# The transfers of two hardware DMA queues, tied in one order: a gated-attention and low-rank-mixer kernel

## The chip, the cores and the metric

The kernel runs on one NeuronCore of a Trainium2 chip. The metric is the device time of one execution in microseconds (us); the time before is the median of five executions. A profile of one of these executions shows each instruction of the engines: TensorE (PE, and PEld for its weight loads), VectorE (DVE), ScalarE (ACT), GpSimd (POOL) and SyncE (SP), and the DMA transfers that SP, ACT and POOL issue.

## The reference

Two blocks run one after the other on eight batches of 3136 rows and 256 columns. The first is a gated attention with squared ReLU, the second a low-rank mixer over the sequence with a two-layer network behind it.

```python
scores = (1.0 / S) * z @ z.T            # z: [8, 3136, 64], S = 3136
attn   = np.maximum(scores, 0.0) ** 2
x      = u * (attn @ v)                 # u, v: [8, 3136, 256]
h      = x.T @ U @ V                    # U: [3136, 32], V: [32, 3136]
y      = x + h.T
out    = y + np.maximum(y @ w_ch1, 0.0) @ w_ch2    # 256 -> 1024 -> 256
```

## The kernel before

The 3136 rows of a batch are 24 blocks of 128 rows and a tail of 64 rows (`NT`, `TAIL`). The scores are symmetric, so a block of the score matrix is computed once; where both it and its transpose are wanted, the second is made by a DMA transpose. Work for one batch runs as follows.

- `load_z`, `cast_z` and `tr_z` (lines 895 to 923) bring z in, scale it to bf16 and transpose it into `zT`. In batch 0 the transpose is a matmul, from batch 1 on a DMA transpose on the SP queue: three of eight blocks, and one for the tail.
- `score` (L1025) multiplies two blocks of `zT` into a pair of PSUM banks. `relu_q` (L1040 on ACT, L1042 on DVE) clips it into SBUF tile `q`, `square` (L1046) squares it, `tr_quad` (L1049) transposes some blocks with a DMA on the SP queue.
- `av` (L1053) multiplies the squared scores by v, which `load_v` (L940) and `cast_v` brought in; `gate` (L1086) multiplies the sum by u, which `load_u` (L967, L970) brought in, and gives x. The tail columns go through `copy_o24` (the copy at L888 into `o`) and a transposing matmul (L1078).
- `t1`, `t1s`, `hmm` (L1095, L1112, L1133) are the low-rank part; `uadd`, `ucast`, `utr` (L1144, L888, L1161) make y and transpose it with a DMA; `w1`, `relu1`, `w2`, `outadd`, `store` (L1171 to L1217) are the two-layer network and the stores.
- Only in batch 0, `load_w` (L978 to L993) and `cast_w` bring the weights in, in between: U and V first, then the two layers' weights.

The work around the change is ordered by a planner. `make_plan` plays the whole kernel through with estimated durations, picks an engine for each task and gives a list of tasks, `plan.order`. The kernel then walks that list under `tc.manual_schedule()`, and each engine executes its own instructions in the order in which they were recorded. Loads are issued from the ACT queue (a few early ones from SP), so they stand in one stream with ScalarE's own instructions; all DMA transposes are issued from SP; stores are issued from POOL, those of the last batch from SP.

```python
    plan = make_plan()
    with tc.manual_schedule():
        bufs = Bufs(tc.nc, ctx, tc, u, v, z, moe_U, moe_V, moe_w_ch1, moe_w_ch2, out)
        for t in plan.order:
            t.emit(bufs, t)
```

How the engines' streams interleave is not fixed by this. The recording layer lays all instructions out in one list of its own. A transfer of SP or ACT takes the next of eight semaphores (`DMAHW0` to `DMAHW7`) as its turn in that list comes, whichever of the two queues it is on; the built program shows it. Each transfer raises its semaphore on landing. So that counts stay clear, a queue waits before it issues a transfer until the previous transfer on the same semaphore, the eighth before it in the list, has landed. On ACT everything behind that transfer waits too. The text below calls this the turn wait. There are 733 such transfers: 487 on SP (458 of them transposes) and 246 on ACT.

Of the kernel before, what the change touches and what calls it, by code (L numbers as in the profile page):

```python
# [15 lines left out]
P = 128  # L16
NB, S, D, DQK, R, H = 8, 3136, 256, 64, 32, 1024
NT = 24
TAIL = S - NT * P
# [17 lines left out]
GATE_V = 0  # L37
# [12 lines left out]
class Ref:  # L50
# [4 lines left out]
    def __init__(self, pool):  # L55
        self.pool, self.i, self.n = pool, None, 0
# [757 lines left out]
class Bufs:  # L814


    def __init__(self, nc, ctx, tc, u, v, z, mU, mV, w1, w2, out):
        self.nc = nc
        self.d = dict(u=u, v=v, z=z, U=mU, V=mV, w1=w1, w2=w2, out=out)
        sb = ctx.enter_context(tc.tile_pool(name="sb", bufs=1))  # L820
        ps = ctx.enter_context(tc.tile_pool(name="ps", bufs=1, space=bass.MemoryType.PSUM))

        def many(name, n, shape, dt):
            return [sb.tile(shape, dt, name=f"{name}{i}") for i in range(n)]

        self.q = sb.tile([P, NBLK, P], BF16, name="q")
        self.xc = many("xc", NXC, [P, 4, D], BF16)
        self.x24 = many("x24_", 2, [P, P], BF16)
        self.stg = many("stg", 6, [P, 512], FP32)
        self.us = many("us", 3, [P, 2, D], FP32)  # L830
        self.zbf = many("zbf", 2, [P, 8, P], BF16)
        self.zbt = sb.tile([P, P], BF16, name="zbt")
        self.zT = many("zT", 2, [P, (NT + 1) * P], BF16)
        self.v = many("v", 2, [P, NT + 2, D], BF16)
        self.TJ = many("TJ", 1, [P, (NT + 1) * 64], BF16)
        self.o24 = many("o24_", 1, [P, P], FP32)
        self.u24 = many("u24_", 1, [P, P], FP32)
        self.u32 = many("u32_", 3, [P, 4, D], FP32)
        self.ubf = many("ubf", 1, [P, ND * 4 * P], BF16)
        self.uT = many("uT", 2, [P, ND * 4 * P], BF16)  # L840
        self.ubt = sb.tile([P, P], BF16, name="ubt")
        self.r1 = many("r1_", 7, [P, 2, 512], BF16)
        self.r24 = many("r24_", 1, [P, NH, 192], BF16)
        self.ob = many("ob", 2, [P, 2, D], FP32)
        self.t1sb = many("t1_", 2, [P, D], BF16)
        self.w1b = sb.tile([P, ND, H], BF16, name="w1b")
        self.w2b = sb.tile([P, NH, D], BF16, name="w2b")
        self.Ub = sb.tile([P, NT + 2, R], BF16, name="Ub")
        self.V4 = sb.tile([P, 6 * P], BF16, name="V4")
        self.Vt = sb.tile([P, 192], BF16, name="Vt")  # L850
        self.t1f = many("t1f", 1, [P, D], FP32)
        self.rep = sb.tile([P, P], FP32, name="rep")
        self.pair = [ps.tile([P, 2, 512], FP32, name=f"pair{i}") for i in range(NPAIR)]
        self.acc = [ps.tile([P, 512], FP32, name=f"acc{i}") for i in range(NACC)]
        self.ident = sb.tile([P, P], BF16, name="ident")
        make_identity(nc, self.ident)
        self.identf = sb.tile([P, P], FP32, name="identf")
        nc.vector.tensor_copy(out=self.identf, in_=self.ident)
        nc.vector.memset(self.zbt[64:], 0.0)
        for t in self.v:  # L860
            nc.vector.memset(t[64:, NT, :], 0.0)
            nc.vector.memset(t[:64, NT + 1, :], 0.0)
        nc.vector.memset(self.r24[0], 0.0)
        nc.vector.memset(self.Ub[64:, NT, :], 0.0)
        nc.vector.memset(self.Ub[:64, NT + 1, :], 0.0)
        nc.vector.memset(self.Vt, 0.0)

    def own(self, x):
# [6 lines left out]
            return q.bitcast(FP32).rearrange("p (t d) -> p t d", d=D)  # L875
        return q

    def q_of(self, t):
        return {"SP": self.nc.sync, "POOL": self.nc.gpsimd, "ACT": self.nc.scalar, "DVE": self.nc.vector}[t.eng]

# [5 lines left out]
    def copy(self, t, out, in_):  # L886
        if t.eng == "ACT":
            self.nc.scalar.copy(out=out, in_=in_)  # L888
        elif t.eng == "POOL":
            self.nc.gpsimd.tensor_copy(out=out, in_=in_)  # L890
        else:
            self.nc.vector.tensor_copy(out=out, in_=in_)  # L892


    def load_z(self, t, b, z0, nb, st):
        s = self.stg[st.i]
        if z0 < NT:
            self.q_of(t).dma_start(
                out=s[:, : nb * DQK].rearrange("p (t d) -> p t d", d=DQK), in_=self.rows("z", b, z0, z0 + nb)
            )  # L900
        else:
            self.q_of(t).dma_start(out=s[:TAIL, :DQK], in_=self.d["z"][b, NT * P :, :])

    def cast_z(self, t, z0, nb, st, zbf, h):
        s = self.stg[st.i]
# [10 lines left out]
    def tr_z(self, t, z0, zbf, zT):  # L916
        if z0 < NT:
            o = self.zT[zT.i][:, z0 * P : (z0 + 8) * P].rearrange("p (t r) -> p t r", r=P)
            i = self.zbf[zbf.i].rearrange("p t c -> p (t c)")
        else:  # L920
            o = self.zT[zT.i][:, NT * P :].rearrange("p (t r) -> p t r", r=P)
            i = self.zbt[:, :]
        self.nc.sync.dma_start_transpose(out=o, in_=i)

    def mm_z(self, t, z0, nb, zbf, pr):
        for n in range(nb):
# [10 lines left out]
    def load_v(self, t, b, k, st):  # L937
        s = self.stg[st.i]
        if k < 12:
            self.q_of(t).dma_start(  # L940
                out=s.rearrange("p (t d) -> p t d", d=D), in_=self.rows("v", b, 2 * k, 2 * k + 2)
            )
        else:
            self.q_of(t).dma_start(out=s[:TAIL, :D], in_=self.d["v"][b, NT * P :, :])

    def load_v_bf(self, t, k, v):
        self.q_of(t).dma_start(
            out=self.v[v.i][:, 2 * k : 2 * k + 4, :], in_=self.rows("v", 0, 2 * k, 2 * k + 4)
        )

    def gate_v(self, t, v):
        w = self.v[v.i]
        self.nc.gpsimd.tensor_copy(out=w[:1, NT // 2, :1], in_=w[:1, 2 * GATE_V, :1])

    def cast_v(self, t, k, st, v):
        s = self.stg[st.i]
# [7 lines left out]

    def load_u(self, t, b, c, u):
        if c < NT:
            self.q_of(t).dma_start(out=self.us[u.i], in_=self.rows("u", b, c, c + 2))  # L967
        else:
            for h in range(2):
                self.q_of(t).dma_start(  # L970
                    out=self.u24[u.i][h * TAIL : (h + 1) * TAIL, :],
                    in_=self.d["u"][b, NT * P :, h * P : (h + 1) * P],
                )

    def load_w(self, t, n, g, st):
        s, q = self.stg[st.i], self.q_of(t)
        if n < 4:
            q.dma_start(out=s, in_=self.d["w1"][n // 2 * P : (n // 2 + 1) * P, n % 2 * 512 : (n % 2 + 1) * 512])  # L978
        elif n < 8:
            d = self.d["w2"][(n - 4) * 2 * P : (n - 3) * 2 * P, :]  # L980
            q.dma_start(out=s.rearrange("p (t d) -> p t d", d=D), in_=d.rearrange("(t p) d -> p t d", p=P))
        elif n < 10:
            t0 = (n - 8) * 12
            q.dma_start(
                out=s[:, : 12 * R].rearrange("p (t r) -> p t r", r=R), in_=self.rows("U", None, t0, t0 + 12)
            )
            if n == 9:
                q.dma_start(out=s[:TAIL, 12 * R : 13 * R], in_=self.d["U"][NT * P :, :])
        else:

            c0 = ((n - 10) * 4 + g) * 504
            w = min(504, S - c0)
            q.dma_start(out=s[g * R : (g + 1) * R, :w], in_=self.d["V"][:, c0 : c0 + w])  # L993

    def cast_w(self, t, n, g, st):
        s = self.stg[st.i]
# [49 lines left out]
        self.nc.vector.tensor_tensor(out=o, in0=o, in1=o, op=ALU.mult)  # L1046

    def tr_quad(self, t, src, off, tb, nt):
        self.nc.sync.dma_start_transpose(out=self.q[:, tb.i : tb.i + nt, :], in_=self.cols(src, off, nt * P))  # L1049

    def av(self, t, seg, acc, v, d0, first, last):
        for n, (_, ref, j) in enumerate(seg):
# [101 lines left out]
    def utr(self, t, k, ubf, uT):  # L1154
        if k < 6:
            i = self.own(ubf)
            o = self.own(uT).rearrange("p (t r) -> p t r", r=P)
        else:
            i = self.ubt[:, :]
            o = self.own(uT)[:, :P].rearrange("p (t r) -> p t r", r=P)  # L1160
        self.nc.sync.dma_start_transpose(out=o, in_=i)  # L1161

    def w1(self, t, k, g, pr, uT):
        ps = self.pair[pr.i]
# [46 lines left out]
    def store(self, t, b, k, h, ob):  # L1211
        if k < 6:
            t0 = 4 * k + 2 * h
            self.q_of(t).dma_start(out=self.rows("out", b, t0, t0 + 2), in_=self.ob[ob.i])  # L1214
        else:
            for e in range(2):
                self.q_of(t).dma_start(  # L1217
                    out=self.d["out"][b, NT * P :, e * P : (e + 1) * P],
                    in_=self.ob[ob.i][e * TAIL : (e + 1) * TAIL, 0, :P],
                )  # L1220
# [3 lines left out]
def kernel(  # L1224
# [9 lines left out]
    out: bass.AP,  # L1234
):
    plan = make_plan()
    with tc.manual_schedule():
        bufs = Bufs(tc.nc, ctx, tc, u, v, z, moe_U, moe_V, moe_w_ch1, moe_w_ch2, out)
        for t in plan.order:
            t.emit(bufs, t)  # L1240
# [30 lines left out]
```

## Time and profile before

| what | value |
|---|---|
| median of five executions | 1041.83 us |
| lowest and highest | 1039.83 and 1047.07 us |
| the profiled execution: its own time | 1040.88 us |
| its span in the trace | 1039.1 us |
| its mean granted TensorE clock | 0.998 |
| busy: PE, PEld | 1009.5 us, 747.0 us |
| busy: DVE, ACT, POOL | 597.7 us, 485.8 us, 72.6 us |
| DMA transposes `q<-q` on SP, issue to landing | 364, median 3.9 us |
| loads of v, 256 KB, on ACT, issue to landing | 84, median 3.6 us |

The time of the profiled execution is 1.78 us more than its span, and 0.95 us less than the median. "Busy" does not count the instructions that only wait or that issue a transfer; those stand under the queue's name (ACTq, SPq). An idle time is shown in brackets behind the instruction that ended it, with what released it.

### The profile page before, as it was taken

The numbers are of one execution on the slowest core, as the hardware profiler recorded it, in microseconds if no ns is written. First come the engines' busy times: TensorE is split into PE (matmuls) and PEld (weight loads), VectorE is DVE, ScalarE is ACT, GpSimd is POOL, SyncE is SP. The second block draws the span as 40 slices with busy tenths as digits, with TensorE's granted clock in tenths as the row PEclk, the third lists the DMA queues.
The fourth block names the chain that finished last, engine by engine and source line by source line (L and its number), as shares of the span: only waits on it lengthen the run. The fifth ranks groups of instructions, "written<-read, shape, count | busy, mean of one in ns | idle before, by whom it ended". The sixth has DMA issues, their size and how long they took to land.

```text
span 1039.1 us, 22175 instructions
## 1 busy us (share of the span) xinstructions
PE 1009.5 (97%) x9103; PEld 747.0 (72%) x9177; DVE 597.7 (58%) x1064; ACT 485.8 (47%) x596; POOL 72.6 (7%) x137
## 2 busy tenths in 40 slices
PE   8798999999999999999999999999999999999997
PEld 5477677777777767777777777677777777777765
DVE  7785754746654566646566554754655655652352
ACT  7553455344545355444454444644464454542343
POOL 1140000000000000001000000000000001000000
PEclk9999999999999999999999999999999999999999
DMA  9989999968797899898699886997889888762152
GB/s 209 172 218 220 185 186 206 202 153 168 167 216 169 166 178 197 182 183 173 139 224 188 188 156 139 212 208 167 166 168 207 195 184 153 136 142 80 40 124 78
DMA packets 413990, 177.84 MB, mean 171 GB/s; under 512 B 375712, under 2 KB 379104, under 8 KB 413888
## 3 DMA queue, kind: packets, MB, share of 16 engines
q1 hardware_dynamic: 372880, 96.91, 55.7%
q10 hardware_dynamic: 33408, 56.25, 19.9%
q0 software_dynamic: 7600, 23.27, 7.2%
q8 instruction: 71, 1.16, 0.5%
q14 instruction: 31, 0.25, 0.1%
HBM read 60.70 MB, written 25.69 MB: 83 GB/s over the span
## 4 chain that ended last, share of the span: by engine, by line
PE 89%; DMA 5%; DVE 3%; ACT 1%; issue 1%; ACTq 0%; POOL 0%; SPq 0%; POOLq 0%; DVEq 0%
PE acc L1053 46%; PE acc L1197 16%; PE pair L1171 15%; PE pair L1025 7%; DMA uT<-ubf 2%; PE acc L1063 2%; DVE q L1046 1%; DMA zT<-zbf 1%; PE pair L1133 1%; PE acc L1068 1%; DMA stg<-in_v_dram 1%; DMA q<-q 1%; PE acc L1190 1%; ACT q L1040 1%; PE acc L1095 1%
## 5 line engine op out<-in xcount | busy, mean ns | idle before, releaser
L1053 PE MATMUL acc<-v,q 128*128 128x256 bf16 x4632 | 572.2, 274 | 4.7 <-DVE xc L1086 4.4
L1053 PEld LDWEIGHTS <-q 128*128 128x128 bf16 x4632 | 441.3, 98 | 123.5 <-issue 50.4
L1040 ACT ACTIVATE q<-pair 128x1024 bf16<-128x1024 f32 (+6 forms) x263 | 214.4, 862 | 220.8 <-PE pair L1025 207.6
L1182 ACT ACTIVATE r<-pair 128x1024 bf16<-128x1024 f32 (+1 forms) x191 | 186.5, 1008 | 185.9 <-PE pair L1171 161.8
L1046 DVE TENSOR_TENSOR q<-q 128x1024 bf16<-128x1024 bf16 (+6 forms) x392 | 211.1, 579 | 14.3 <-ACT q L1040 13.5
L1086 DVE TENSOR_TENSOR xc<-acc,us 128x256 bf16<-128x256 f32 x192 | 81.0, 422 | 192.6 <-PE acc L1053 96.7
L1197 PE MATMUL acc<-w2b,r 128*128 128x256 bf16 x1536 | 182.4, 273 | 0.0
L1171 PE MATMUL pair<-uT,w1b 128*128 128x512 bf16 (+1 forms) x716 | 165.7, 350 | 5.7 <-DMA uT<-ubf 2.0
L1197 PEld LDWEIGHTS <-r 128*128 128x128 bf16 x1536 | 149.0, 98 | 24.3 <-issue 4.0
L1042 DVE TENSOR_SCALAR q<-pair 128x768 bf16<-128x768 f32 (+6 forms) x129 | 125.1, 975 | 52.5 <-PE pair L1025 48.2
L1171 PEld LDWEIGHTS <-w1b 128*128 128x128 bf16 x896 | 78.5, 98 | 70.8 <-issue 5.4
L1209 DVE TENSOR_TENSOR ob<-acc,u 128x512 f32<-128x512 f32 (+1 forms) x91 | 60.0, 659 | 86.4 <-PE acc L1197 85.8
L1214 POOL DMA_DIRECT2D out_dram<-ob x84 | 46.7, 556 | 849.2 <-DVE ob L1209 804.9
L1025 PE MATMUL pair<-zT 64*128 64x384 bf16 (+3 forms) x952 | 100.8, 314 | 4.4 <-ACT q L1040 3.1
L1025 PEld LDWEIGHTS <-zT 64*128 64x128 bf16 x952 | 35.8, 95 | 35.1 <-issue 25.6
L1144 DVE TENSOR_TENSOR u<-pair,xc 128x1024 f32<-128x1024 f32 x42 | 50.1, 1218 | 9.6 <-PE pair L1133 9.6
L888 ACT CAST ubf<-u 128x1024 bf16<-128x1024 f32 x23 | 24.0, 1045 | 61.1 <-DVE u L1144 54.1
L892 DVE CAST v<-stg 128x512 bf16<-128x512 f32 (+1 forms) x69 | 28.1, 409 | 18.7 <-DMA stg<-in_v_dram 17.8
L1063 PE MATMUL acc<-v,q 64*128 64x256 bf16 (+1 forms) x168 | 27.0, 277 | 0.0
L912 ACT ACTIVATE zbf<-stg 128x512 bf16<-128x512 f32 (+1 forms) x34 | 19.8, 615 | 10.5 <-DMA stg<-in_z_dram 10.0
L1171 PE MATMUL pair<-q,w1b 128*128 128x512 bf16 (+1 forms) x106 | 22.0, 351 | 1.6 <-DVE q L1144 1.0
L1063 PEld LDWEIGHTS <-q 64*128 64x128 bf16 (+1 forms) x168 | 11.3, 95 | 11.7 <-issue 10.3
(71 smaller groups left out, 242.3 us busy)
## 6 DMA issues: line engine op xcount, KB each, us to landing
us<-in_u_dram ACTq DMA_DIRECT2D x93, 256.0 KB, 3.5
stg<-in_v_dram ACTq DMA_DIRECT2D x84, 256.0 KB, 3.6
out_dram<-ob POOLq DMA_DIRECT2D x84, 256.0 KB, 3.1
q<-q SPq DMA_TRANSPOSE x364, 3.9
stg<-in_z_dram ACTq DMA_DIRECT2D x22, 256.0 KB, 3.2
out_dram<-ob SPq DMA_DIRECT2D x12, 256.0 KB, 2.0
stg<-in_moe_w_ch_dram ACTq DMA_DIRECT2D x8, 256.0 KB, 3.5
stg<-in_v_dram SPq DMA_DIRECT2D x6, 256.0 KB, 3.8
```

Source lines behind the costliest of these rows:

```text
L1025: self.nc.tensor.matmul(out=ps[:, h, pc : pc + w], lhsT=z[a, r * P : (r + 1) * P], rhs=z[a, c0 : c0 + w], start=True, stop=True,)
L1040: self.nc.scalar.activation(out=o, in_=i, func=AF.Relu)
L1042: self.nc.vector.tensor_single_scalar(out=o, in_=i, scalar=0.0, op=ALU.max)
L1046: self.nc.vector.tensor_tensor(out=o, in0=o, in1=o, op=ALU.mult)
L1053: self.nc.tensor.matmul(out=self.acc[acc.i][:, d0 : d0 + D], lhsT=self.q[:, ref.i, :], rhs=self.v[v.i][:, j, :], start=first and n == 0, s ...
L1063: self.nc.tensor.matmul(out=a[:, :D], lhsT=q[r], rhs=v[r, NT + n, :], start=n == 1, stop=n == 0)
L1086: self.nc.vector.tensor_tensor(out=o, in0=i0, in1=i1, op=ALU.mult)
L1144: self.nc.vector.tensor_tensor(out=o, in0=i, in1=x, op=ALU.add)
L1171: self.nc.tensor.matmul(out=o, lhsT=self.w1b[:, e, ht * P : (ht + 1) * P], rhs=r, start=e == 0, stop=e == ND - 1)
L1182: self.nc.scalar.activation(out=o, in_=i, func=AF.Relu)
L1197: self.nc.tensor.matmul(out=self.acc[acc.i][:, w * D : (w + 1) * D], lhsT=self.r1[r1s[ht // 2].i][:, ht % 2, (2 * h + w) * P : (2 * h + w ...
L1209: self.nc.vector.tensor_tensor(out=o, in0=i, in1=x, op=ALU.add)
```

## The change

All transfers of SP and ACT, loads, stores and transposes alike, go through a new method `chain`. It adds an edge from each to the one recorded before it, whichever queue that was on. The edge is of the kind `NoSync`: it orders the two in the recording layer's list and puts no wait on the chip. The eight semaphores thus come round in the order of `plan.order`. POOL is taken out of the manual schedule, and each of its instructions is tied to the one recorded before it on POOL by `keep_in_program_order`.

```diff
-        self.nc = nc
+        self.nc, self.tc, self.last = nc, tc, None
...
+    def dma(self, t, out, in_):
+        i = self.q_of(t).dma_start(out=out, in_=in_)
+        if t.eng == "POOL":
+            self.tc.keep_in_program_order(i)
+        else:
+            self.chain(i)
+
+    def chain(self, i):
+        if self.last is not None:
+            self.tc.add_manual_dep(
+                i.ins, self.last.ins.name, mybir.DependencyInfo(mybir.DependencyClass.NoSync, mybir.DependencyReason.DATA),
+                reason="order of transfers",
+            )
+        self.last = i
...
-            self.nc.gpsimd.tensor_copy(out=out, in_=in_)
+            self.tc.keep_in_program_order(self.nc.gpsimd.tensor_copy(out=out, in_=in_))
...
-            self.q_of(t).dma_start(
+            self.dma(t, 
                 out=s.rearrange("p (t d) -> p t d", d=D), in_=self.rows("v", b, 2 * k, 2 * k + 2)
             )
...
-        self.nc.sync.dma_start_transpose(out=self.q[:, tb.i : tb.i + nt, :], in_=self.cols(src, off, nt * P))
+        self.chain(self.nc.sync.dma_start_transpose(out=self.q[:, tb.i : tb.i + nt, :], in_=self.cols(src, off, nt * P)))
...
-    with tc.manual_schedule():
+    E = mybir.EngineType
+    with tc.manual_schedule(engines={E.PE, E.Activation, E.DVE, E.SP}):
```

The other loads, stores and transposes are wrapped in the same way.

## The prediction

> **What bounds the kernel now.** I read the page first, then busy time by stretches of the first 120 us, then the timelines of PE and ACT there, then the chain.
>
> ```profile
> PE 1009.5 (97%) x9103; PEld 747.0 (72%) x9177; DVE 597.7 (58%) x1064; ACT 485.8 (47%) x596; POOL 72.6 (7%) x137
> PE   8798999999999999999999999999999999999997
> PE 89%; DMA 5%; DVE 3%; ACT 1%; issue 1%; ACTq 0%; POOL 0%; SPq 0%; POOLq 0%; DVEq 0%
> ```
>
> PE is the bound: 97% busy, in a chain that is 89% PE. A change in the order of semaphores takes no matmul away, so it can win only where PE stands idle. Summing PE's gaps over 0.15 us in the trace gives 20.5 us, of which 4.0 are the start. Between 120 and 1035 us only four reach 0.7 us, and none 0.9. What can be moved lies between 30 and 120 us, in batch 0 and at the passage to batch 1: about 11 us.
>
> ```profile
> 44.00:48.00 4.00, 0.92 (x8) 0.84 (x9) 0.97 (x3) 0.27 (x1) 0.99 (x3) 1.00 1.20 221
> 48.00:52.00 4.00, 4.00 (x24) 2.25 (x22) 2.96 (x5) 2.38 (x3) 3.79 (x6) 0.58 0.29 70
> ...
> 82.00:84.00 2.00, 2.00 (x20) 1.79 (x19) 0.00 (x0) 0.00 (x0) 0.00 (x0) 1.00 1.29 81
> ...
> 94.00:96.00 2.00, 2.00 (x40) 1.46 (x38) 1.12 (x3) 0.30 (x1) 0.00 (x0) 1.00 1.05 391
> ...
> 112.00:116.00 4.00, 2.54 (x40) 1.57 (x40) 2.61 (x8) 3.71 (x5) 0.00 (x0) 1.00 1.29 193
> ```
>
> Columns: length, busy time of PE, PEld, DVE, ACT and POOL, granted clock, DMA share, GB/s. PE works 0.92 us of four at 44, and in the next four has 0.58 of its clock. The DMA share is 0.8 to 1.4 in the rows from 76 to 96 and over 1 from 100 to 116: transfers queue there.
>
> ```profile
> 42.13 4.54 ACTq L993 DMA_DIRECT2D stg<-in_moe_V_dram  x2
> 46.76 0.27 ACT L888 COPY o<-acc 128x128 f32<-128x128 f32 x1 [6.20 <-DMA stg<-in_moe_V_dram]
> ```
>
> ```profile
> 47.08 0.33 PE L1078 MATMUL acc<-identf,o 128*128 128x128 f32 x1 [3.30 <-ACT o L888]
> ```
>
> The second V load on ACT (L993) issues at 46.35, 0.02 us after the landing of an unrelated `q<-q` transpose, the eighth transfer before it: the turn wait. It needs nothing else. The copy of `o` behind it on ACT is late, and PE stands 3.30 us.
>
> ```profile
> 79.49 9.67 ACTq L940 DMA_DIRECT2D stg<-in_v_dram  x3
> ```
>
> ```profile
> 79.12 9.14 DMA zT<-zbf
> 88.26 0.02 issue
> 88.28 0.02 ACTq L940
> 88.30 0.04 issue
> 88.34 0.33 ACTq L940
> ```
>
> The same, longer: the second v load could go at 79.92, waits for a z transpose to land at 88.26, goes at 88.34. The chain runs through that wait.
>
> ```profile
> 93.32 1.25 PE L1053 MATMUL acc<-v,q 128*128 128x256 bf16 x10 [1.65 <-DVE xc L1086]
> 94.50 0.85 PE L1025 MATMUL pair<-zT 64*128 64x64 bf16 x27
> ...
> 113.36 0.99 PE L1025 MATMUL pair<-zT 64*128 64x384 bf16 x6 [1.43 <-ACT q L1040]
> ```
>
> What PE pays there: 1.65 us at 91.7, 1.43 at 112, where two u loads (L970) hold ACT with turn waits of 2.2 and 3.0 us.
>
> **The change part by part.** I laid the two built programs beside each other and their waits on the times of this trace. No engine's own order changes. Of the 733 transfers 233 change their place in the list of turns, by up to four. What changes is which landing each transfer waits for.
>
> *Removed.* Turn waits that held ACT over 0.1 us add up to 39.8 us before: 26.1 of it from 40 to 117 us, nine waits, and 13.7 in 14 short ones from 170 to 788 us, where PE has no gap to give back. I value the latter at nothing: ACT is idle 220.8 us before L1040 alone. Carrying the new waits through the trace's own durations leaves 16.1 us on ACT.
>
> *Added.* SP, which had 1.8 us of them, gets 10.3. On the old times nine transfers would be issued before the landing they now wait for: six on SP, 15.5 us, three on ACT, 3.7 us. Largest is 4.45 us, for a `q<-q` transpose at 83.8 us that must now let a z transpose land; queued behind it on SP are the third z transpose and the z tail's, and PE's scores at 94.50 wait for the tail. Twenty-two more pure wait instructions on ACT and DVE, four fewer on SP, at some 0.05 us each in this trace, are 1.1 us on engines with 53% and 42% idle: nothing. POOL's order is unchanged, and its stores land behind everything: nothing. If those covers were gone they would cost at most that 1.1 us.
>
> The sum, on PE:
>
> 1. At 44 us. The V load now waits for a transpose that landed at 41.69; it issues at 42.4, the copy of `o` ends at 43.07 instead of 47.02, and the 3.30 us gap closes. But the *next* V load takes over that turn, for the same landing at 46.33, and holds the `relu` behind it: done at 48.21, not 49.18. The scores at 49.87 need it. PE does its 16 matmuls ahead of them and stands again, from about 45.1 to 48.3. Gain: 49.87 − 48.3 = 1.6 us. The clock record has the half rate from 47.98 to 51.39 us. [...] By the row the gap only moves by 1.3 us, and the window from 44.56 to 47.98 still holds next to no work, so I leave the half rate where it is. Then 3.1 instead of 1.5 us of score-and-product time falls into it: 0.8 us back. Net −0.8.
> 2. At 53 us. A u load (L967) was held 4.04 us for a transpose landing at 56.81; its new predecessor landed at 50.5. The casts of U and two `relu` come earlier; PE's 0.64 us gap at 58.8 and smaller waits behind it go: −1.5, so −2.3.
> 3. At 80 us. The v load goes at about 78 instead of 88.3, and PE's 1.65 us at 91.7 is gone. But PE cannot start the scores of the tail before the z tail has landed, and that moves hardly at all: SP's new waits take what the earlier start gave. At 96 us PE is only 0.4 ahead: +1.9.
> 4. At 106 to 117 us. The turn waits before the u loads (2.2, 3.0, then 1.9 us) go; PE's 0.41, 1.43 and two waits of 0.38 go: −2.9, so −3.3.
>
> This takes every transfer's time to landing as it was. [...] By the row, DMA is at 1.29 share and 81 GB/s around 82 us. A 256 KB load at the 391 GB/s of the row at 94 us is 0.67 us of all engines. One load moves wholly ahead of the z transposes, others partly. With 0 added per transpose the sum stays −3.3, with 0.5 us it is −2.3, with 1 us −1.3: transposes late are paid twice, in SP's turn waits and again in landing. I take 0.5, nearest to that one load. After 120 us PE has hardly a gap, so a head start there lasts to the end.
>
> Result −2.3 us against this execution's 1040.88, that is 1038.6. The execution lies 0.95 under the median; on the median it is 1039.5.
>
> **The rivals.**
>
> *More is won: the gap and the half clock both go.* [...] With no half rate the same working gives −4.9; if the earlier loads also let SP's transposes spread, up to −7. Against it: the new gap is worked out at 3.1 us in nearly the same place. Time about 1036.
>
> *Slower: the z tail.* One mechanism: at 77 to 90 us the loads released early share the engines with three z transposes; the `q<-q` transpose waits for one of them, SP stops, and the tail's transpose, last in SP's line, lands late. Each microsecond that every transpose there takes longer costs PE two. At 1.6 us more the whole gain is gone; at 3 us the sum is +2.8. For it: the z transposes take 7 to 9 us here already, against a median of 4.1. Against: the load brought wholly forward is worth 0.67 us. Time about 1044, and the decision falls at 1.6 us.
>
> *It does nothing.* If the list had already run in plan order, nothing would move. The programs exclude that; but the gains at 44 and 80 us could all be given back at the next wait, as steps 1 and 3 half show. Time 1041.8.
>
> **How the numbers follow.** Forecast 0.58, more won 0.2, nothing 0.1, slower 0.12. The range 1034.5 to 1044.5 reaches from −7 to +3: it takes in both ends of the contention and the repeat spread of this kernel (1039.83 to 1047.07). A measurement of this kernel tells about 0.5%, 5.2 us, from no change: under 1036.6 is faster, over 1047.0 slower. The forecast is mostly between; of the rival that wins more a good half is beyond. That gives faster 0.17, same 0.76, slower 0.07.
>
> **What would show it.** Right: ACT's idle before the copy of `o` near 43 us under 2.5 us, and a new gap of 2 to 3.5 us before PE's next scores; the half-clock stretch still there; the v loads at 77 to 79 us no longer 9 us apart; SP standing about 4 us before a `q<-q` transpose near 82; PE's scores of batch 1's tail at 94 to 96 us; no gap over 0.7 us at 108 to 117; PE's idle 2 to 4 us less in all. Wrong: a clock record without the half stretch (the first rival), z transposes of 10 us and tail scores after 97 us (the second), or any PE gap over 1 us after 120 us, where I expect nothing.

## The result, and the profile after

The changed kernel takes 1040.33 us (median of 43 executions, 1033.67 to 1045.68) against 1044.04 us before (80 executions, 1038.95 to 1054.97). The ratio is 0.9964, with a 95% interval of 0.9952 to 0.9975: 3.7 us less, with 2.6 and 5.0 as the ends. That is under the 0.5% that the prediction counted as no change. The larger sample of before lies 2.2 us above the five executions of the opening table, so the difference, not the time, is what the forecast of −2.3 us is held against.

The two profiled executions say the opposite of the medians. The one of the change took 1042.55 us (span 1040.8), 2.2 us above its own median; the one of before took 1040.88 us, 3.2 us under its own. Their totals can't be compared; their places can. In the changed kernel L1040, L1025, L1053 and L1078 have become L1058, L1043, L1071 and L1096, and every load is issued at L879.

The page of the changed kernel, busy time and the shares of the chain:

```profile
PE 1011.5 (97%) x9103; PEld 748.5 (72%) x9177; DVE 598.1 (57%) x1064; ACT 486.1 (47%) x596; POOL 72.0 (7%) x137
PE   8897999999999999999999999999999999999998
PE 92%; DMA 4%; DVE 2%; issue 1%; ACT 1%; ACTq 0%; POOL 0%; SPq 0%; DVEq 0%; POOLq 0%
```

PE is still the bound. It is busy 2.0 us longer than before for the same 9103 matmuls; its mean granted clock is 0.993, against 0.998.

The same view by stretches (length, busy time of PE, PEld, DVE, ACT and POOL, granted clock, DMA share, GB/s):

```profile
44.00:48.00 4.00, 3.08 (x28) 2.30 (x27) 2.28 (x4) 0.06 (x1) 1.42 (x4) 1.00 1.50 138
48.00:52.00 4.00, 2.85 (x18) 2.10 (x18) 2.86 (x5) 2.24 (x3) 3.78 (x6) 0.78 0.71 149
...
92.00:96.00 4.00, 0.00 (x0) 0.00 (x0) 0.43 (x1) 0.00 (x0) 0.00 (x0) 0.83 1.14 228
96.00:100.00 4.00, 3.61 (x38) 2.56 (x39) 1.82 (x2) 2.59 (x4) 0.00 (x0) 0.50 0.43 137
112.00:116.00 4.00, 4.00 (x38) 2.56 (x35) 3.19 (x7) 1.75 (x3) 0.00 (x0) 1.00 1.40 153
```

The hole at 44 us is mostly filled (3.08 us of PE instead of 0.92) and the one at 112 us wholly (4.00 instead of 2.54). A new one of four whole microseconds has opened at 92, and in the next four the granted clock is 0.50.

The timeline of ACT in the changed kernel:

```profile
43.80 0.27 ACT L905 COPY o<-acc 128x128 f32<-128x128 f32 x1 [2.16 <-PE acc L1086]
46.17 1.86 ACTq L879 DMA_DIRECT2D stg<-in_moe_V_dram  x2
48.08 1.02 ACT L1058 ACTIVATE q<-pair 128x1024 bf16<-128x1024 f32 x1 [4.02 <-issue]
```

and that of PE:

```profile
44.69 0.27 PE L1096 MATMUL acc<-identf,o 128*128 128x128 f32 x1
49.16 0.32 PE L1043 MATMUL pair<-zT 64*128 64x384 bf16 x2 [2.08 <-ACT q L1058]
...
96.39 1.44 PE L1043 MATMUL pair<-zT 64*128 64x64 bf16 x27 [4.44 <-DMA zT<-zbt]
...
115.49 0.71 PE L1043 MATMUL pair<-zT 64*128 64x384 bf16 x6
```

The copy of `o` now waits for PE, not for a landing, and the matmul behind it comes at 44.69 instead of 47.08. The V load that follows it has taken over the turn and goes at 46.17. The row holds two loads; the second takes 1.51 us to issue, where the same load takes 0.43 us in a second profile of the change (f1, below). So the `relu` starts at 48.08, 1.1 us later than the turn alone would make it, and PE stands 2.08 us before its next scores. Near 113 us nothing is waited for. At 92 us PE waits 4.44 us for the transposed z tail. SP's timeline says why that is late:

```profile
79.46 9.91 SPq L1067 DMA_TRANSPOSE q<-q  x3
89.46 1.27 SPq L940 DMA_TRANSPOSE zT<-zbf  x1
90.82 1.24 SPq L940 DMA_TRANSPOSE zT<-zbt  x1
```

Three `q<-q` transposes take SP 9.91 us, 5.71 of it one turn wait (82.47 to 88.24), and the z tail's transpose is last in that line.

### The profile page after: what moved, and what is told of

Its sections match the earlier page's. It is cut to its first block, busy times and chain, and to the rows that moved or that the text cites. A ratio compares the mean times of both kernels' runs of the same rounds, so it can differ in the third digit from the quotient of the medians.

```text
span 1040.8 us, 22193 instructions
## 1 busy us (share of the span) xinstructions
PE 1011.5 (97%) x9103; PEld 748.5 (72%) x9177; DVE 598.1 (57%) x1064; ACT 486.1 (47%) x596; POOL 72.0 (7%) x137
## 3 DMA queue, kind: packets, MB, share of 16 engines
q8 instruction: 71, 1.16, 0.5%
## 4 chain that ended last, share of the span: by engine, by line
PE 92%; DMA 4%; DVE 2%; issue 1%; ACT 1%; ACTq 0%; POOL 0%; SPq 0%; DVEq 0%; POOLq 0%
PE acc L1071 47%; PE acc L1215 16%; PE pair L1189 16%; PE pair L1043 8%; DMA uT<-ubf 2%; PE acc L1081 2%; PE acc L1086 1%; PE pair L1151 1%; PE acc L1113 1%; PE acc L1208 1%; DMA zT<-zbt 1%; DMA q<-q 0%; DMA stg<-in_v_dram 0%; DVE q L1162 0%; DVE q L1064 0%
## 5 line engine op out<-in xcount | busy, mean ns | idle before, releaser
L1071 PE MATMUL acc<-v,q 128*128 128x256 bf16 x4632 | 574.6, 275 | 4.2 <-DVE xc L1104 3.3
L1071 PEld LDWEIGHTS <-q 128*128 128x128 bf16 x4632 | 442.5, 98 | 124.5 <-issue 48.1
L1058 ACT ACTIVATE q<-pair 128x1024 bf16<-128x1024 f32 (+6 forms) x263 | 214.6, 861 | 230.1 <-PE pair L1043 217.5
L1104 DVE TENSOR_TENSOR xc<-acc,us 128x256 bf16<-128x256 f32 x192 | 81.1, 422 | 195.0 <-PE acc L1071 98.9
L879 POOL DMA_DIRECT2D out_dram<-ob x98 | 54.4, 556 | 877.4 <-DVE ob L1227 832.8
L1043 PE MATMUL pair<-zT 64*128 64x384 bf16 (+3 forms) x952 | 101.0, 316 | 7.6 <-DMA zT<-zbt 4.4
L1043 PEld LDWEIGHTS <-zT 64*128 64x128 bf16 x952 | 35.8, 95 | 38.1 <-issue 28.6
L929 ACT ACTIVATE zbf<-stg 128x512 bf16<-128x512 f32 (+1 forms) x34 | 19.8, 615 | 10.0 <-DMA stg<-in_z_dram 9.6
L1058 ACT ACTIVATE TJ<-pair 128x1024 bf16<-128x1024 f32 (+1 forms) x10 | 9.4, 947 | 25.6 <-PE pair L1043 25.6
```

What stands on the lines that cost most here:

```text
L879: i = self.q_of(t).dma_start(out=out, in_=in_)
L1043: self.nc.tensor.matmul(out=ps[:, h, pc : pc + w], lhsT=z[a, r * P : (r + 1) * P], rhs=z[a, c0 : c0 + w], start=True, stop=True,)
L1058: self.nc.scalar.activation(out=o, in_=i, func=AF.Relu)
L1071: self.nc.tensor.matmul(out=self.acc[acc.i][:, d0 : d0 + D], lhsT=self.q[:, ref.i, :], rhs=self.v[v.i][:, j, :], start=first and n == 0, s ...
L1104: self.nc.vector.tensor_tensor(out=o, in0=i0, in1=i1, op=ALU.mult)
```

## The experiments

All are timed against the kernel before on the same chip. "Turn waits" are counted as in the prediction, on ACT and on SP. The ratios are the recorded comparison of all executions of a row with those of before; they are not the quotients of the two medians, and the two can differ: for e10 the ratio makes 9.1 us less, the medians 7.7; for e8 they make 7.6 and 9.6 us more. The change was timed 43 times, most others 14 or 22 times, but e10 and e11 11 times, e7 9, e8 8 and e9 only 2.

| label | what it is | us | before | ratio (95%) | turn waits ACT / SP, us |
|---|---|---|---|---|---|
| before | | 1044.04 | | | 39.8 / 1.8 |
| after | the change | 1040.33 | 1044.04 | 0.9964 (0.9952 to 0.9975) | 17.2 / 13.2 |
| f1_change_again | the change | 1040.67 | 1044.11 | 0.9963 (0.9946 to 0.9981) | 20.0 / 10.1 |
| e3_until_130 | early turns only | 1042.56 | 1043.84 | 0.9981 (0.9965 to 0.9997) | 23.9 / 11.1 |
| f2_until_130_again | the same | 1043.76 | 1044.11 | 0.9995 (0.9977 to 1.0014) | 25.5 / 12.4 |
| e4_from_130 | late turns only | 1042.65 | 1043.84 | 0.9988 (0.9974 to 1.0003) | 30.1 / 1.6 |
| f3_from_130_again | the same | 1044.36 | 1044.11 | 1.0008 (0.9989 to 1.0026) | 29.7 / 1.4 |
| e5_tail_first | change, z tail loaded first | 1044.04 | 1043.84 | 1.0000 (0.9972 to 1.0027) | |
| e7_warm | change, PE kept busy at 90 us | 1038.57 | 1043.84 | 0.9946 (0.9923 to 0.9969) | 24.5 / 15.3 |
| e8_late4 | loads up to 4 turns later | 1052.07 | 1042.51 | 1.0073 (1.0046 to 1.0101) | 87.9 / 0 |
| e9_early6 | loads up to 6 turns earlier | 1087.84 | 1042.51 | 1.0417 (1.0356 to 1.0477) | 0.4 / 239.8 |
| e10_early80 | first 80: loads one turn earlier | 1034.82 | 1042.51 | 0.9913 (0.9883 to 0.9943) | 15.5 / 14.0 |
| e11_early80_warm | e10 with PE kept busy | 1036.11 | 1042.51 | 0.9928 (0.9903 to 0.9954) | 14.1 / 14.0 |
| f4_early_there_and_late | e10, and one earlier from the 135th on | 1039.40 | 1044.11 | 0.9941 (0.9920 to 0.9962) | 12.7 / 12.1 |

**Where the change acts: the early turns and the late ones.** The plan's start time of a task decides whether its transfer gets an edge: before 130 us (66 turns change) or after (167).

```diff
-        if self.last is not None:
+        if self.last is not None and self.tied:
...
         for t in plan.order:
+            bufs.tied = -1.0 <= t.start < 130.0     # e4: 130.0 <= t.start
             t.emit(bufs, t)
```

> The transfers are tied in plan order only up to the planner's 130 us; 66 transfers change their turn as in the change, the later 167 keep the turn they had before. My theory (all of the gain is made at PE's idle times between 40 and 120 us, and the rest of the program has nothing to give back): the whole gain, 3.7 us less than before (2.5 to 5). Rival (many short turn waits later on add up): half of it or less, 0 to 1.8 us. In the profile: ACT's wait before the copy of o near 43 us under 2.5 us, and a wait of SP of 4 us or more before a q transpose near 82 us.

> The reverse: the first 66 turns as before, the 167 from the planner's 130 us on in plan order. My theory: no change, within 1 us of before, although ACT's turn waits after 130 us become fewer. Rival (later turn waits count): 2 us or more faster. In the profile: the 3.3 us gap of PE near 44 us and the long turn wait of a v load near 80 us are both there as before.

The two ratios lie inside each other's intervals, so both halves and the change were timed again, side by side.

> The change itself once more, beside its two halves on the same chip, and for a second profile of it. Theory: 0.4% faster than before, and in the profile a PE gap of 1 to 3 us before the scores near 47 us and of 3 to 5 us before the tail scores near 92 us. If the first profile was an accident of one execution, the gap near 92 us is under 2 us here.

> Plan order up to the planner's 130 us only, repeated because 0.2% (0.03 to 0.35) left open whether that is the whole gain. If the first 66 turns carry it all: 0.3 to 0.4%. If a third belongs to the later turns: 0.2 to 0.25%.

> Plan order from the planner's 130 us on only, repeated because 0.12% (-0.03 to 0.26) could not be told from nothing. If the first 66 turns carry the gain: under 0.1%. If a third belongs to the later turns: 0.1 to 0.2%.

The change repeats (−3.4 us by the medians). Its early half gives 0.4 and 1.3 us, its late half nothing that can be told from zero. My theory that the early turns carry the whole gain was a miss in the times: e3 and f2 lie under the 2.5 to 5 us that it asked for. The traces say more on what the early turns do, because a gap has a place. PE's waits in five places, in us, a dash where under 0.6:

| executions | at 43 to 46, before `o`'s transpose | near 48, scores | near 60, scores | near 92, tail scores | near 113, scores |
|---|---|---|---|---|---|
| early turns as before (before, e4, f3) | 3.30, 2.14, 2.15 | – | 0.67, 2.23, 1.79 | – | 1.43, 2.26, 0.98 |
| early turns in plan order (after, f1, e3, f2) | –, 1.16, –, – | 2.08, –, 1.06, 1.87 | – | 4.44, 4.43, 3.90, 4.87 | – |
| e10 | – | – | – | 0.76 | – |

In every execution with the early turns in plan order the waits near 60 and 113 us are gone and the one before the tail's scores is there; in none of the three others. The wait at 43 to 46 us is gone, or 1.16 us in f1, and a smaller one has come near 48. Which places the early turns change is shown by four traces against three; what the places are worth together is not shown by this. PE's timeline in the second profile of the change (f1) has the wait for the z tail at the same length within 0.01 us, so it is no accident of one execution:

```profile
93.59 1.43 PE L1043 MATMUL pair<-zT 64*128 64x64 bf16 x27 [4.43 <-DMA zT<-zbt]
```

**Can the wait for the z tail be taken away by its order?** Batch 1's z tail is loaded and transposed first, not last; the rest is planned anew.

```diff
+        if b == 1:
+            pieces = ((NT, 1), (0, 8), (8, 8), (16, 8))
```

> The change, and in batch 1 the tail piece of z is loaded, scaled and transposed first instead of last, so that it is not last in SP's line. The planner works the whole order out anew. My theory (step 3: what the change wins at 80 us is given back because the z tail lands late and PE's tail scores wait for it): PE's gap before the tail scores (4.4 us in the profile after) falls under 1.5 us, and the half-clock stretch behind it goes with it: 3 to 6 us faster than the change, that is 6 to 10 us faster than before. Rival (the DMA engines are full there, any order only moves the wait to the other z transposes or to v): PE stands as long near 92 us for something else, within 1.5 us of the change.

With a ratio of 1.0000 the gain of the change is gone. The planner's new order differs in other places too, so the total can't be put down to the tail alone; the wait can be followed. It did not go; PE now waits for another z transpose. PE's timeline, SP's timeline, and SP's own waits between 80 and 92 us (for what: us in total, times, longest us):

```profile
96.64 1.03 PE L1045 MATMUL pair<-zT 64*128 64x64 bf16 x11 [5.71 <-DMA zT<-zbf]
```

```profile
78.32 10.47 SPq L1069 DMA_TRANSPOSE q<-q  x3
88.88 1.26 SPq L942 DMA_TRANSPOSE zT<-zbf  x1
```

```profile
SPq L1069 <- DMA zT<-zbf: 4.9, 1, 4.9
```

It is the same turn wait as in the change: the third `q<-q` transpose has its turn behind the second z transpose, which lands 11.53 us after its issue (76.08 to 87.61), and holds SP for 4.9 us. The third z transpose stands behind it on SP, is issued at 88.88 and lands at 96.59, 7.71 us later. The tail was only the last in that line. For the z tail's order as the cause this is a miss; the turn wait in front of it is what makes the line late.

**What is the lower clock behind that wait worth?** 28 matmuls whose result nothing reads fill PE's wait, in the change and in e10.

```diff
+        if t.name == "it1.24.0":
+            for n in range(28):
+                self.nc.tensor.matmul(
+                    out=ps[:, 0, :D], lhsT=self.w1b[:, 0, :P], rhs=self.w1b[:, 1, :D], start=True, stop=True
+                )
```

> The change, and 28 extra matmuls of 256 columns (3.1 us at full clock) on PE in front of batch 1's tail scores, into a bank that the scores then overwrite; they do nothing but keep PE active in its gap there. If the half clock behind the gap costs 2 to 3 us, as the two half-rate windows at 94.6 us in the profile after say: 1.5 to 3 us faster than the change, the clock record without the stretch near 95 us. If the gap is often shorter than in that one profile, or the half rate comes anyway: the same as the change or up to 2 us slower.

```profile
93.30 3.22 PE L1043 MATMUL pair<-w1b 128*128 128x256 bf16 x28
96.69 0.84 PE L1048 MATMUL pair<-zT 64*128 64x64 bf16 x27 [0.17 <-DMA zT<-zbt]
```

The tail's scores come at 96.69 (96.39 in the change), but take 0.84 us instead of 1.44, and the 15 product matmuls behind them 1.81 us, against 3.38 in f1: the clock stays up. Both profiles of the change have a half-rate stretch of 6.83 us there (94.63 to 101.46; 92.3 to 99.1), this one has none after 90 us. But one of its two stretches, at 85.69, is where neither profile of the change has one, behind a wait of 2.19 us. By the ratios it takes 1.9 us less than the change, in the range expected, but the two intervals overlap, so the time leaves it open; the trace shows that the stretch behind the tail's wait goes.

**The turn itself as the dose.** The strongest test leaves the work and every engine's order as in the change and moves only the turns of ACT's loads in the list. The edges are laid once at the end, along a list `TURNS` of all 733 transfers.

```diff
+        self.all.append(i)
...
+    def tie(self):
+        for a, b in zip(TURNS, TURNS[1:]):
+            self.tc.add_manual_dep(self.all[b].ins, self.all[a].ins.name, ...)
...
+TURNS[37:42] = [38, 39, 40, 41, 37]     # e10: 16 such pieces, all among the first 81
+TURNS[42:45] = [43, 44, 42]
...
```

> Every instruction, and the order on every engine, as in the change; only the list of turns differs: each load on ACT takes its turn up to four places later than in plan order, as far as the data dependencies allow (1.5 places on the mean; before the change it was 0.4). My theory (the list matters because a transfer waits for the landing of the one eight turns before it, and ACT's own work waits behind it): ACT's turn waits rise from 40 us before to about 93 us, SP's fall to nothing, and the time is 10 to 20 us more than before (16 by carrying the new waits through the durations of the trace before). Rival (the gain of the change was something else, such as the phase of the clock, and turn waits are mostly covered): within 3 us of before.

> The opposite end: each load on ACT takes its turn up to six places earlier than in plan order. ACT has then hardly a turn wait left (about 1 us), but a transpose on SP may have to let a load land that is issued after it would be: SP's turn waits rise to about 250 us. My theory (a turn wait costs on whichever queue it falls, on SP through late transposes): 35 to 60 us slower than before. Rival (only ACT matters, since SP does nothing else): as fast as the change or faster.

> The change, and among the first 80 transfers each load on ACT takes its turn one place earlier than in plan order (51 transfers change their place by one or so); the rest in plan order. By the trace before, this takes the turn wait of the second V load near 46 us away, which in the change still holds ACT, and closes PE's gap before the scores at 47 us. My theory: 7 us less than before (5 to 8), 2 to 4 less than the change; in the profile no PE gap over 1 us between 43 and 60 us. Rival (the gap moves on once more, as in the change): within 1.5 us of the change.

With later turns the loads wait for landings that are more recent, and the waits pile up on ACT (87.9 us, none on SP); with earlier turns the transposes wait for the loads, on SP (239.8 us, 0.4 on ACT). Both ends cost: +7.6 us and +43.5 us by the ratio. The second was expected (35 to 60), the first is under the 10 to 20 expected, but its interval excludes the rival's 3 us. With loads four later, PE stands before its scores in the same stretch (PE's timeline of e8):

```profile
59.72 1.04 PE L1153 MATMUL pair<-zT 64*128 64x512 bf16 x4 [2.38 <-ACT q L1168]
62.86 0.61 PE L1153 MATMUL pair<-zT 64*128 64x512 bf16 x2 [2.11 <-ACT q L1168]
```

With loads six earlier, SP's own waits (engine and line, for what: us in total, times, longest us) are for loads:

```profile
SPq L1099 <- DMA stg<-in_v_dram: 90.9, 39, 6.9
SPq L1099 <- DMA us<-in_u_dram: 54.7, 28, 5.2
```

and PE stands 7.78 us before the tail's scores:

```profile
106.57 1.46 PE L1075 MATMUL pair<-zT 64*128 64x64 bf16 x27 [7.78 <-DMA zT<-zbt]
```

Between the ends lies a better place than the plan's own. In e10, 51 of the first 80 transfers are moved, each load by one turn. It is the fastest kernel here, 9.1 us under before by the ratio (5 to 8 expected). ACT's timeline, PE's and SP's:

```profile
44.56 0.79 ACTq L898 DMA_DIRECT2D stg<-in_moe_V_dram  x2
45.40 1.02 ACT L1079 ACTIVATE q<-pair 128x1024 bf16<-128x1024 f32 x1 [2.08 <-DMA q<-q]
```

```profile
43.95 0.27 PE L1117 MATMUL acc<-identf,o 128*128 128x128 f32 x1
44.06 1.80 PE L1092 MATMUL acc<-v,q 128*128 128x256 bf16 x15
45.79 1.00 PE L1064 MATMUL pair<-zT 64*128 64x512 bf16 x6
...
89.03 0.84 PE L1064 MATMUL pair<-zT 64*128 64x64 bf16 x27 [0.76 <-DMA zT<-zbt]
```

```profile
75.28 5.21 SPq L1088 DMA_TRANSPOSE q<-q  x3
80.83 3.37 SPq L961 DMA_TRANSPOSE zT<-zbf  x1
84.66 1.12 SPq L961 DMA_TRANSPOSE zT<-zbt  x1
```

The V load behind the copy goes at 44.56 instead of 46.17 (46.10 in f1), the `relu` starts at 45.40 instead of 48.08 (46.94 in f1), and PE has no gap from 39 to 60 us. On SP the turn wait of 5.71 us before the third `q<-q` transpose is 0.44 us. Both hold in all three profiles with these early turns: e10, and e11 and f4 below, have no PE wait over 0.6 us between 43 and 60 us, and no turn wait over 1.1 us on SP between 75 and 85 us, where the change, e3, f2, e5 and e7 have one of 4.5 to 5.7 us. The sums of turn waits do not tell e10 from the change (15.5 and 14.0 against 17.2 and 13.2 us): it matters which transfer waits.

> The kernel of the run with the first 80 turns one place earlier, and in addition the 28 extra matmuls in front of batch 1's tail scores. If PE still waits 3 us or more there and the half clock follows, another 1 to 2.5 us less, 8 to 10 less than before. If the earlier turns have shortened that wait to under 2 us, the extra matmuls cost up to 2 us instead.

No gain over e10 that can be told: in e10's profile PE stands only 0.76 us there, and the 28 matmuls take 3.22 us themselves.

> As the run with the first 80 turns of ACT's loads one place earlier, and from the 135th transfer on one place earlier too (378 transfers change their place against the change). If turn waits after 130 us cost nothing, since PE has no gap there: the same as that run, 0.8 to 0.9% less than before. If they do: another 0.1 to 0.3%.

It moves the late loads by one turn too. It is not better than e10 (on another chip, so the two are compared only through before): 6.2 us less than before by the ratio, where the same as e10 was expected. Its profile has a wait of 3.61 us on `uT<-ubf` at 567 us, where the profile of before has 0.25; but f3 has 1.76 us there, the change 1.92 in one profile and 0.21 in the other, so one profile does not put it down to the late turns. Its early turns are e10's, and yet the tail's scores wait:

```profile
91.91 1.37 PE L1199 MATMUL pair<-zT 64*128 64x64 bf16 x27 [3.11 <-DMA zT<-zbt]
```

Here it is the landing: the tail's transpose takes 8.13 us, against 4.24 in e10 and 6.19 in e11. The early turns take the waits at 44 to 60 us and on SP away each time; that the tail's scores hardly wait is one execution of e10, itself 4.3 us faster than its median.

## Why the prediction was right or wrong

The direction, the bound and the places of the steps held; the size came out 1.4 us too small, and some of the signs fell. To compare places across executions whose clock differs, I take half of PE's busy time in half-rate stretches away from the time at which an event comes:

| event, us, as measured and (corrected) | before | after | f1 |
|---|---|---|---|
| tail's scores of batch 1 start | 94.50 (92.8) | 96.39 (93.0) | 93.59 (93.6) |
| first `t1` matmul with `t1f` of batch 0 starts | 117.2 (115.5) | 118.7 (112.8) | 116.1 (113.4) |
| between them | 22.7 (22.7) | 22.3 (19.8) | 22.5 (19.8) |
| PE's idle time up to the second | 16.6 | 15.8 | 15.2 |

The correction is rough. It takes work in such a stretch to last twice as long; the 15 product matmuls behind the tail's scores take 3.38 us at half rate in f1 and 1.81 us at full rate in before. The same 907 matmuls up to the second event, so corrected, still take 96.2 to 98.9 us of busy time in the seven executions, so it carries up to 2.7 us that is neither waiting nor half rate. PE's idle time is the plainer measure.

- **Step 1, at 44 us**: right in kind. In the profile after, ACT's idle time before the copy was 2.16 us (under 2.5), the gap moved behind the next V load as worked out, and the scores came at 49.16 and, in f1, at 48.02, for a forecast 48.3. In f1 the copy still came late: the V load before it had a turn wait of 1.3 us, ACT was idle 4.06 us and 1.16 us of the first gap was left. The new gap is smaller than the 3.1 us worked out: 2.08, 0.51, 1.06 and 1.87 us in after, f1, e3 and f2. The two larger ones are those in which the second V load took 1.51 and 1.23 us to issue, not 0.43; why, the traces don't show. The half-rate stretch was left in its place, for 0.8 us of loss, by the row of one execution, in which PE was busy 0.90 us of the 3.42 before it: the author's estimate. With the same early turns, after and f2 have one there (50.26, 49.05), f1 and e3 have none.
- **Step 2, at 53 us**: right. The wait near 60 us is under 0.6 us in all four executions, against 0.67, 2.23 and 1.79 in the others; the 1.5 us of the step can't be told apart from the rest.
- **Step 3, at 80 us**: right in kind. SP stood 5.71 us (forecast about 4) before a `q<-q` transpose at 82, and PE's wait of 1.65 us became one of 4.4 us further on. By the corrected time the tail's scores come at 93.0, 93.6, 91.1 and 92.3 us in the four executions, at 92.8, 92.2 and 92.1 in the three others: level, so what had been won was given back. The working had PE 0.4 us ahead and then took 1 us off for contention: 0.6 behind. This is where the slower rival's mechanism was at work: between 70 and 100 us of the profile after, SP's transfers took 41.1% and ACT's 52.7% of the time of the 16 DMA engines. One of its two signs came, a z transpose of 10.43 us (10.16 in f1); the other, tail scores after 97 us, did not (96.39, and 93.59 in f1). Up to half a microsecond per transpose fits these times; the 1.6 at which the whole gain would be gone does not. The half microsecond behind that 1 us was the author's estimate, which no run shows by itself: to landing, the three z transposes and the tail's took 7.04, 9.14, 3.95 and 4.75 us before, 7.62, 10.43, 6.58 and 5.43 in the profile after.
- **Step 4, at 106 to 117 us**: right, with a price that it left out. The forecast gain was 2.9 us; between the two events the corrected time fell by 2.9 in both profiles. But the half rate behind the tail's new wait falls into this stretch, so as measured it fell by only 0.4 and 0.1 us. Step 3 named that wait and put no clock on it.
- **The sum**: the forecast was −2.3 us. By the corrected time of the first `t1` matmul, the four executions with plan-order early turns (112.8, 113.4, 111.0, 112.1) lie 2.4 us before the three others (115.5, 114.6, 114.1). By PE's idle time up to there it is 1.9 us (15.8, 15.2, 14.2, 15.7 against 16.6, 16.9, 17.8). By the times as measured it is only 0.7 (means 116.8 and 117.5), since all four run at half rate behind the tail's wait (0.22 to 0.23 us for each of the first product matmuls there, against 0.12 in the three others). The medians of all executions give −3.7, and even the near end of their interval, 2.6, is over the forecast. So at least 1.3 us is not found in the four steps, and which term was too small stays open. That the forecast came near is in part luck.
- **PE's idle time in all**: a miss. The sign was 2 to 4 us less; span less busy time makes 29.6 us before, 29.3 after and 27.8 in f1.
- **Behind 120 us**: the value of nothing for the late turns is neither refuted nor shown. Alone they measure 1.3 us or less either way. But the halves together give about −1.4 us, with an uncertainty of 1.8, where the whole gives −3.8 with 1.1. Whether the rest is the two acting together or scatter stays open. "No PE gap over 1 us after 120" was wrong: after has 1.92 us at 570.5, f2 2.56 us in the same place, both on a `uT<-ubf` transpose; f1 has 0.21 there.
- **POOL and the extra waits at nothing**: for POOL this is settled by the built program. With the edges left out, and POOL still taken out of the manual schedule and tied, it has the same instructions with the same waits as before. So POOL's part is nothing; the edges are the change.
- **"More is won"** needed an execution without both gap and half rate near 48 us. f1 and e3 come near it (waits of 1.16 and 0.51 us, and of 1.06 us; no half rate there), but behind the tail's wait they run at half rate (15 product matmuls in 3.38 and 3.35 us); e10 has neither, by other turns. Its −4.9 us was the sum before the 1 us for the transposes; with it, it is −3.9. **"It does nothing"** is excluded by the interval.

## What to carry to other kernels

Two queues share eight semaphores here: a load stood until the transfer eight turns earlier had landed (8.4 us, from 79.92 to 88.34, in the profile before), and so did everything behind it on its engine. Where a trace shows this, the order in which the transfers are recorded is a resource. Look in the timeline for a DMA issue that takes microseconds and ends at the landing of an unrelated transfer, and move that one turn. The list as a whole in plan order moved much of the wait to the other queue here (ACT 39.8 to 17.2 us, SP 1.8 to 13.2). When a wait goes, name the next one in line and its place, and hold the places, not two single totals, against each other.

## What the runs showed of the hardware

- Single executions of one kernel differ by more than the change is worth: before spans 1038.95 to 1054.97 us. Part of it is the clock: among the 67 executions of before beside f1, the fastest (1037.23 us) has a mean granted clock of 0.998, one of 1051.92 us 0.991.
- The SP and ACT transfers of before and after are spread over eight semaphores, 91 or 92 on each. In each of the two, all 725 that follow another on their semaphore were issued at least 0.02 us after that one had landed. The traces show the wait, not its reason.
- Half-rate stretches are 3.41 us or a multiple of it (6.83, in e9 once 10.24). Leaving out those at the very end, before has one at 47.98; after at 33.19, 50.26 and 94.63; f1 only at 92.3; e10 only at 31.82. In all 34 such stretches of the 14 profiles PE was busy for at most 1.74 of the 3.41 us directly before; in after 1.74, 1.34 and 0.74 us. No single wait of 3.41 us was needed: before the first of these PE's longest wait was 1.53 us.
- A PE wait of 4.4 us cost twice: once as standing time, and again as half the clock over the 5.1 us (after) or 5.5 us (f1) of work behind it, by estimate half of that, some 2.5 to 2.8 us.
- A z transpose, which the prediction had at a median of 4.1 us to landing, took 10.43 us in after, 11.53 in e5 and 11.37 in e10, each with loads of v issued while it was under way.
